# A GpSimd cast put on ScalarE in two of eight MLP steps of a long-convolution and ELU-MLP kernel

## The chip, the cores and the metric

The kernel runs on one core of one Trainium2 chip. The metric is the device time of one execution in microseconds, as the median of several runs. A core has a matrix engine (TensorE, PE in the profile; its weight loads are shown apart as PEld), VectorE (DVE), ScalarE (ACT), GpSimd (POOL) and SyncE (SP), which here only issues DMAs. Each engine takes its instructions in the order in which the program issues them, and waits on semaphores where an operand comes from another engine.

## What is computed

The reference convolves a gated signal with a long generated filter (by FFT, over 12480 positions, 4 batches, 128 channels), gates the result with x, and puts each of the 49920 rows through an MLP with an ELU:

```python
h_filt = (np.maximum(pos_emb @ w1, 0.0) @ w2) * np.exp(-0.01 * pos)[:, None]
u = x * v
y = irfft(rfft(u, n=2 * S, axis=1) * rfft(h_filt, n=2 * S, axis=0)[None], n=2 * S, axis=1)[:, :S]
t = (x * y).reshape(B * S, D)                      # 49920 x 128
h = t @ w_in                                       # 128 -> 2048
g = np.where(h > 0.0, h, np.exp(np.minimum(h, 0.0)) - 1.0)
out = g @ w_out                                    # 2048 -> 128
```

## The kernel before

**Precision.** Every matmul operand is split in two parts, a high one rounded to the format fp32r (`_h`) and the rest (`_l`). A product is then three matmuls, `hi*hi`, `hi*lo` and `lo*hi` (`mm3`, lines 53 to 55). So each operand costs a cast, which rounds it, and a subtraction, which makes the rest. For the MLP's activations g these are line 575 (`g_h`, a cast on GpSimd) and line 581 (`g_l = g - g_h`, on VectorE). The helper `copy` (line 57 and 58) is a ScalarE activation with the function Copy; all its uses show as L58.

**Stages.** First the weights are prepared and the forward and inverse FFT of batch 0 are done (about 530 us, with the filter's own transform in between). Then comes the MLP of all four batches, and beside the MLP of batch p, for p = 0, 1, 2, the FFT work of batch p + 1 (`stage1`, `stage2`), cut into small units that a generator yields. The MLP of batch 3 stands alone.

**The MLP.** It runs over 120 blocks of 416 rows (30 to a batch, batch by batch), and in each block over eight steps c = 0 to 7; a step handles 256 of the 2048 hidden columns. `run` (line 499) writes the order out by hand; what a step s issues, in this order, is:

- `up_proj(s)`: six matmuls into the PSUM tile `fps`, of which there are two; then two ScalarE activations, `n = relu(-h)` (L565) and `n = exp(-n)` (L566), each over 128 x 832;
- `split_lo(s - 2)`: `g_l` (L581, VectorE);
- `elu(s)`: `g = max(n - 1, h)` on VectorE (L572), which is the last reader of `fps`; then the cast `g_h` (L575, GpSimd);
- `down_proj(s - 4)`: six matmuls that add to the PSUM tile `ops`, of which there is one. After the last step of a block, so in the step with c = 3 of the next block, ScalarE copies `ops` to `o_sb` (L58). The next step opens the accumulation of the next block in the same PSUM tile;
- one or two units of the next batch's FFT (`SHARE = 1.08`): ScalarE copies, VectorE products and splits, GpSimd additions (`p<-p`, L431 and L432), matmuls into the two PSUM tiles of `psx`;
- things done once a block: c = 0 the inverse transform of the next block (`conv_out`) and the loads of the one three ahead; c = 1 a store; c = 2 `split_b(j + 2)`; c = 3 `transp(j + 1)`, with the ScalarE copy `t_h` and the VectorE subtraction `t_l`; c = 6 `finish(j - 1)`.

**What is special in batch 0.** Its inverse FFT was written in one part, so `split_b` makes the two parts on the core: a ScalarE copy `b<-b` of 104 x 1024 (L527 in the code, L58 in the profile) and a GpSimd subtraction (L529, also `b<-b`). For the later batches both parts come from memory and `split_b` does nothing.

**Buffers** that the steps below touch: `fps` 2, `ops` 1, `psx` 2, the tile `m` for `conv_out`, `transp` and `finish` 1; in SBUF n 2, g 3, `g_h` and `g_l` 5 each.

Of the kernel before, what the change touches and what calls it, by code (L numbers as in the profile page):

```python
# [38 lines left out]
def fftconv_gate_elu_mlp_kernel(ctx: ExitStack, tc: tile.TileContext, x, v, pos_emb, w1, w2,  # L39
                                w_in, w_out, dft, ident, window, tab, out):  # L40
    nc = tc.nc
# [15 lines left out]
    def copy(out, in_):  # L57
        nc.scalar.activation(out=out, in_=in_, func=ACTF.Copy)  # L58
# [427 lines left out]
    class Mlp:  # L486
# [12 lines left out]
        def run(self, side, alone):  # L499
            blocks = [(b, w, n) for b in range(NB) for w in range(2) for n in range(NG)]  # L500
# [68 lines left out]
            def elu(j, c):  # L569
                ps, n = gs[j, c]  # L570
                g = self.ep.tile([128, 2, NT], F32, tag="g", name="g", bufs=3)
                nc.vector.scalar_tensor_tensor(out=g, in0=n, scalar=-1.0, in1=ps[:, :, :NT],  # L572
                                               op0=ALU.add, op1=ALU.max)
                g_h = self.gp.tile([128, 2, NT], F32R, tag="g_h", name="g_h")
                nc.gpsimd.tensor_copy(out=g_h, in_=g)  # L575
                gs[j, c] = (g, g_h)

            def split_lo(j, c):
# [49 lines left out]
            for s in range(len(steps) + LAG):  # L628
# [7 lines left out]
                if now:  # L636
                    elu(*now)
# [9 lines left out]
                if now:  # L647
                    j, c = now
# [107 lines left out]
```

## Time and profile before

| | us |
|---|---|
| median of 3 runs | 3546.19 (3544.32 to 3550.76) |
| profiled execution, its time | 3553.1 |
| span of the profiled execution, first to last instruction | 3551.3 |
| mean granted TensorE clock | 0.981 |
| MLP steps of batch 0, first to last g | about 530 to 1346 from the span's start |

The rows quoted below come from that one profiled execution. A row of a group reads: line, engine, operation, tile written <- tiles read, shapes, count, then busy us and mean ns of one, then the idle time of the engine just before these instructions and what ended it. A row of the timeline reads: start in us from the span's start, length in us, engine, line, operation, tiles, shapes, and in square brackets the engine's idle time before it with what ended it. A row of the waits reads: who waited, for whom, us in total, times, longest. Line numbers are those of the kernel before.

### The profile page before, as it was taken

To read this page: it belongs to the slowest core of one execution; us is meant where nothing else is said; L and a number is where in the kernel's file an instruction comes from. 1 tells how busy PE (TensorE), PEld (TensorE's weight loads), DVE (VectorE), ACT (ScalarE), POOL (GpSimd) and SP (SyncE) were. 2 spreads that over 40 slices of the span, in tenths; PEclk is the share of its full clock that TensorE was granted. 3 is DMA by queue.
4 is the path that set the end of the run, shared out by engine and by line. 5 is a ranking of instruction groups with operands and counts; after the bars stand their busy time and mean duration, and the time that the engine had idled before them with its cause. 6 is when DMAs were issued, how large, how long until landed. Compare 5 with 4: busy or idle time off the path is not lost.

```text
span 3551.3 us, 53404 instructions
## 1 busy us (share of the span) xinstructions
PE 3394.7 (96%) x18444; PEld 3131.3 (88%) x18444; DVE 3114.3 (88%) x3897; ACT 2410.1 (68%) x3290; POOL 2355.2 (66%) x1622
## 2 busy tenths in 40 slices
PE   7978879999999999999999999999999999999999
PEld 5667758889989998889999998899999999999998
DVE  4549969999999989999999989999999988888887
ACT  3445548766666677876666677776666677777776
POOL 5758857667767766557677656666766656565565
PEclk9879979999999999999999999999999999999999
DMA  6758887667767616778888846778888832222221
GB/s 187 236 170 268 269 245 222 203 175 217 214 191 215 192 50 182 242 213 228 230 241 225 230 124 183 239 215 237 232 240 226 230 102 60 71 59 64 67 59 27
DMA packets 383995, 646.30 MB, mean 182 GB/s; under 512 B 24678, under 2 KB 170438, under 8 KB 374366
## 3 DMA queue, kind: packets, MB, share of 16 engines
q1 hardware_dynamic: 383305, 642.73, 63.8%
q8 instruction: 147, 2.41, 0.3%
q14 instruction: 122, 1.00, 0.1%
q10 hardware_dynamic: 421, 0.16, 0.0%
HBM read 412.76 MB, written 230.03 MB: 181 GB/s over the span
## 4 chain that ended last, share of the span: by engine, by line
PE 59%; DVE 10%; DMA 7%; issue 4%; ACT 1%; POOL 1%; SPq 1%; POOLq 0%; DVEq 0%; ACTq 0%
PE fps L53 8%; PE fps L55 8%; PE fps L54 8%; PE ops L53 7%; PE ops L54 7%; PE ops L55 7%; DMA al<-a_d 3%; DVE g_l L581 3%; PE bps L450 3%; DVE g L572 2%; DMA vt<-in_v_dram 2%; PE xps L53 2%; PE xps L55 2%; PE xps L54 2%; PE yps L53 1%
## 5 line engine op out<-in xcount | busy, mean ns | idle before, releaser
L575 POOL CAST g_h<-g 128x832 fp32r<-128x832 f32 x960 | 1228.3, 1283 | 961.0 <-DVE g L572 960.1
L565 ACT ACTIVATE n<-fps 128x832 f32<-128x832 f32 x960 | 831.9, 867 | 737.9 <-PE fps L55 725.1
L572 DVE SCALAR_TENSOR_TENSOR g<-n,fps 128x832 f32<-128x832 f32 x960 | 974.4, 1015 | 224.2 <-ACT n L566 218.2
L581 DVE TENSOR_TENSOR g_l<-g,g_h 128x832 fp32r<-128x832 f32 x960 | 1111.4, 1158 | 18.3 <-POOL g_h L575 18.3
L566 ACT ACTIVATE n<-n 128x832 f32<-128x832 f32 x960 | 864.6, 901 | 30.4
L53 PE MATMUL fps<-t_h,wi_h 128*128 128x416 f32 x1920 | 715.8, 373 | 22.1 <-DVE g L572 20.9
L53 PE MATMUL ops<-g_h,wo_h 128*128 128x416 f32 x1920 | 677.9, 353 | 0.8 <-ACT o_sb L58 0.3
L54 PE MATMUL ops<-g_l,wo_h 128*128 128x416 f32 x1920 | 675.2, 352 | 0.7 <-DVE g_l L581 0.7
L55 PE MATMUL fps<-t_h,wi_l 128*128 128x416 f32 x1920 | 675.8, 352 | 0.0
L55 PE MATMUL ops<-g_h,wo_l 128*128 128x416 f32 x1920 | 675.8, 352 | 0.0
L54 PE MATMUL fps<-t_l,wi_h 128*128 128x416 f32 x1920 | 675.0, 352 | 0.0
L431 POOL TENSOR_TENSOR p<-p 120x768 f32<-120x768 f32 x204 | 478.9, 2348 | 77.9 <-DVE p L425 58.4
L53 PEld LDWEIGHTS fps<-t_h,wi_h 128*128 128x128 f32 x1920 | 362.4, 189 | 55.9 <-DVE g L572 36.1
L54 PEld LDWEIGHTS fps<-t_l,wi_h 128*128 128x128 f32 x1920 | 364.4, 190 | 13.3 <-DVE t_l L554 0.3
L53 PEld LDWEIGHTS ops<-g_h,wo_h 128*128 128x128 f32 x1920 | 361.8, 188 | 7.1 <-POOL g_h L575 2.1
L54 PEld LDWEIGHTS ops<-g_l,wo_h 128*128 128x128 f32 x1920 | 362.5, 189 | 4.2 <-DVE g_l L581 1.4
L55 PEld LDWEIGHTS ops<-g_h,wo_l 128*128 128x128 f32 x1920 | 361.5, 188 | 4.1
L55 PEld LDWEIGHTS fps<-t_h,wi_l 128*128 128x128 f32 x1920 | 361.8, 188 | 3.2
L423 DVE TENSOR_TENSOR p<-xps,f 120x512 f32<-120x512 f32 x416 | 283.0, 680 | 14.1 <-DMA f<-f_d 5.1
L432 POOL TENSOR_TENSOR p<-p 120x256 f32<-120x256 f32 x204 | 249.5, 1223 | 16.0
L450 PE MATMUL bps<-p,t 120*120 120x256 f32 x832 | 220.4, 387 | 35.4 <-POOL p L432 26.6
L358 DVE TENSOR_TENSOR tl<-t,th 120x360 fp32r<-120x360 f32 x208 | 211.2, 1016 | 27.4 <-ACT th L58 27.3
(96 smaller groups left out, 4946.2 us busy)
## 6 DMA issues: line engine op xcount, KB each, us to landing
a_d<-a_sb SPq DMA_DIRECT2D x90, 832.0 KB
al<-a_d SPq DMA_DIRECT2D x156, 480.0 KB
f<-f_d SPq DMA_DIRECT2D x312, 240.0 KB
b_d<-b_sb SPq DMA_DIRECT2D x156, 480.0 KB
b<-b_d SPq DMA_DIRECT2D x90, 832.0 KB
t<-in_tab_dram SPq DMA_DIRECT2D x208, 281.2 KB
xt<-in_x_dram SPq DMA_DIRECT2D x60, 416.0 KB
vt<-in_v_dram SPq DMA_DIRECT2D x60, 416.0 KB
```

Source lines behind the costliest of these rows:

```text
L53: nc.tensor.matmul(out=ps, lhsT=hi, rhs=bh, start=start, stop=False)
L54: nc.tensor.matmul(out=ps, lhsT=hi, rhs=bl, start=False, stop=False)
L55: nc.tensor.matmul(out=ps, lhsT=lo, rhs=bh, start=False, stop=stop)
L423: nc.vector.tensor_tensor(out=p[:, :, :2], in0=ps[:, :, 0:1, :].to_broadcast([RI, TG, 2, D]), in1=f[:, :, r], op=ALU.mult)
L431: e.tensor_tensor(out=q, in0=q, in1=p, op=ALU.add)
L432: e.tensor_tensor(out=q[:, :, 1], in0=q[:, :, 1], in1=q[:, :, 2], op=ALU.add)
L450: nc.tensor.matmul(out=ps[:, o], lhsT=t[:, o, 3 * N2:], rhs=y[:, o, :2], start=True, stop=True)
L565: nc.scalar.activation(out=n, in_=ps[:, :, :NT], func=ACTF.Relu, scale=-1.0)
L566: nc.scalar.activation(out=n, in_=n, func=ACTF.Exp, scale=-1.0)
L572: nc.vector.scalar_tensor_tensor(out=g, in0=n, scalar=-1.0, in1=ps[:, :, :NT], op0=ALU.add, op1=ALU.max)
L575: nc.gpsimd.tensor_copy(out=g_h, in_=g)
L581: nc.vector.tensor_tensor(out=g_l, in0=g, in1=g_h, op=ALU.subtract)
```

## The change

In `elu`, for blocks of batch 0 and the steps c = 2 and c = 3, the cast of g is issued as a ScalarE copy in place of the GpSimd cast. It keeps its place in the program: right after the VectorE instruction that makes g, ahead of `down_proj`, of the FFT units and of `split_b` or `transp` of the same step. All other steps keep the cast on GpSimd. 60 of 960 casts are moved.

```diff
@@ -572,7 +572,10 @@
                 nc.vector.scalar_tensor_tensor(out=g, in0=n, scalar=-1.0, in1=ps[:, :, :NT],
                                                op0=ALU.add, op1=ALU.max)
                 g_h = self.gp.tile([128, 2, NT], F32R, tag="g_h", name="g_h")
-                nc.gpsimd.tensor_copy(out=g_h, in_=g)
+                if blocks[j][0] == 0 and c in (2, 3):
+                    copy(g_h, g)
+                else:
+                    nc.gpsimd.tensor_copy(out=g_h, in_=g)
                 gs[j, c] = (g, g_h)
```

## The prediction

> **What bounds the kernel now.** I read the page first, for how full each engine is, then the busy time by stretches, for where the first batch's MLP differs from the later ones.
>
> ```profile
> PE 3394.7 (96%) x18444; PEld 3131.3 (88%) x18444; DVE 3114.3 (88%) x3897; ACT 2410.1 (68%) x3290; POOL 2355.2 (66%) x1622
> ...
> L575 POOL CAST g_h<-g 128x832 fp32r<-128x832 f32 x960 | 1228.3, 1283 | 961.0 <-DVE g L572 960.1
> ```
>
> TensorE (PE) is the engine that is nearly always busy. ScalarE (ACT) and GpSimd (POOL) are both about two thirds busy, and the cast of g on POOL usually waits for VectorE (DVE) to make g. The averages invite the change: neither engine looks full. The stages say more. First the instructions that make g, 240 to a batch, then all engines in stretches: the middle of batch 0 (blocks 1 to 24, with the FFT of batch 1 beside them), its last five blocks (no FFT left), and the middle of batch 2. Columns: busy us and count of each engine, clock, DMA share, GB/s.
>
> ```profile
> 530.00:1346.60 816.60, 242.90 (x240) 0.99 0.67 186
> ...
> 2141.70:2933.00 791.30, 243.33 (x240) 1.00 0.75 212
> ```
>
> ```profile
> 555.00:1240.00 685.00, 654.10 (x3618) 612.25 (x3618) 663.49 (x803) 478.53 (x641) 498.50 (x330) 1.00 0.73 204
> 1240.00:1346.00 106.00, 105.24 (x561) 99.66 (x561) 88.21 (x93) 80.30 (x100) 71.89 (x44) 1.00 0.27 71
> ...
> 2160.00:2830.00 670.00, 660.43 (x3660) 621.13 (x3661) 632.87 (x810) 473.79 (x637) 442.47 (x308) 1.00 0.81 230
> ```
>
> Batch 0 takes 816.6 us and batch 2, with the same MLP, 791.3: 25.3 us more. In the middle of batch 0, DVE is busy 663.5 of 685 us (97%) and PE idles 685 - 654.1 = 30.9 us, 1.3 us in each of 24 blocks; in batch 2 it idles 9.6 us of 670. So there is something to win in batch 0, at most about those 30.9 us. What PE waits for there, and the mean length of the matmul that opens an up projection beside that of one inside it:
>
> ```profile
> PE fps L53 <- DVE g L572: 14.6, 16, 1.5
> ...
> PE ops L53 <- ACT o_sb L58: 0.3, 1, 0.3
> ```
>
> ```profile
> L53 PE MATMUL fps<-t_h,wi_h 128*128 128x416 f32 x387 | 146.8, 379 | 14.7 <-DVE g L572 14.6
> ...
> L54 PE MATMUL fps<-t_l,wi_h 128*128 128x416 f32 x386 | 135.9, 352 | 0.0
> ```
>
> Half of the idle time is the up projection waiting for g, which frees its PSUM buffer; the wait for o_sb is next to nothing. A matmul that had to wait is also recorded longer: 379 against 352 ns, 27 ns x 387 = 10.4 us, 0.4 us a block. So PE has about 1.3 + 0.4 = 1.7 us a block in the middle that a delay can fall into, and 106 - 105.24 = 0.76 us in all five last blocks together.
>
> **The change, part by part.** I write 13.2 for step c=2 of block 13. Sixty casts (30 blocks, steps 2 and 3) leave POOL and become ACT copies. POOL loses 60 x 1.28 us; that by itself is worth nothing to the end, since POOL is busy 73% in this stretch. The copy's price: no row shows 128x832 from g, but the second activation below has that shape, both ends in SBUF, and takes 0.90 us; the bounds are the 0.50 us of o_sb (416 columns) and the 1.04 us of b (1024 columns, 104 partitions). I take 0.9.
>
> The copy's wait decides more than its length. It is issued straight behind n of the same step, and must wait until DVE has made g from that n. ACT then does nothing, and everything behind the copy stands: at step 2 the copy b<-b for block j+2 and the next step's n; at step 3 o_sb, the FFT's copies, t_h and the next n. Here is ACT, then DVE, POOL and PE around steps 13.2 and 13.3 (start, length):
>
> ```profile
> 908.57 0.90 ACT L566 ACTIVATE n<-n 128x832 f32<-128x832 f32 x1
> 909.37 1.04 ACT L58 ACTIVATE b<-b 104x1024 fp32r<-104x1024 f32 x1
> 910.66 0.87 ACT L565 ACTIVATE n<-fps 128x832 f32<-128x832 f32 x1 [0.24 <-PE fps L55]
> 911.56 0.90 ACT L566 ACTIVATE n<-n 128x832 f32<-128x832 f32 x1
> 912.36 0.50 ACT L58 ACTIVATE o_sb<-ops 128x416 f32<-128x416 f32 x1
> 912.76 0.59 ACT L58 ACTIVATE b_sb<-bps 120x512 fp32r<-120x512 f32 x1
> 913.23 0.52 ACT L58 ACTIVATE t_h<-tps 128x416 fp32r<-128x416 f32 x1
> 914.18 0.87 ACT L565 ACTIVATE n<-fps 128x832 f32<-128x832 f32 x1 [0.43 <-PE fps L55]
> ```
>
> ```profile
> 909.76 1.01 DVE L572 SCALAR_TENSOR_TENSOR g<-n,fps 128x832 f32<-128x832 f32 x1
> ...
> 912.56 1.01 DVE L572 SCALAR_TENSOR_TENSOR g<-n,fps 128x832 f32<-128x832 f32 x1
> ...
> 916.95 1.75 DVE L358 TENSOR_TENSOR tl<-t,th 120x360 fp32r<-120x360 f32 x1
> ```
>
> ```profile
> 910.84 0.88 POOL L575 CAST g_h<-g 128x832 fp32r<-128x832 f32 x1 [2.12 <-DVE g L572]
> ...
> 915.11 3.20 POOL L529 TENSOR_TENSOR b<-b,b 104x1024 fp32r<-104x1024 f32 x1
> ```
>
> ```profile
> 913.98 0.35 PE L53 MATMUL ops<-g_h,wo_h 128*128 128x416 f32 x1
> ...
> 915.83 0.35 PE L53 MATMUL fps<-t_h,wi_h 128*128 128x416 f32 x1
> ```
>
> ACT has only 0.24 us idle between its first n here and the n of 914.18, bar 0.43 at the end: steps 2 and 3 are the two in which ACT is locally full, with b, o_sb and t_h. Replay, with starts spaced as in the rows (0.8 behind an n, 0.95 behind b, 0.4 behind o_sb) and 0.1 us from DVE to the next engine (910.77 to 910.84 above): g 13.2 ends at 909.76 + 1.01 = 910.77; the copy starts at 910.85 instead of b at 909.37; b at 911.65; n 13.3 at 912.6 (was 910.66), its second half ends at 914.4; g 13.3 runs from 914.45 to 915.45 (was 912.56 to 913.57); the second copy starts at 915.55; o_sb at 916.35 (was 912.36), ending at 916.85. The first matmul of the next output accumulation, at 913.98 now, writes the single PSUM buffer that o_sb empties. It starts at 916.9: PE stalls 2.9 us, in a place where it had 913.98 - 912.86 = 1.1 us to spare.
>
> What is late next: t_h at about 917.2 instead of 913.2, n 13.4 at 917.7 or later instead of 914.18, and so g 13.4 at 919.5 to 920 against 916.01. Its consumer, the up projection of 13.6, has itself been pushed 2.9 us by PE's own stall, so this is mostly the same delay and not a second one. The tables and loads in SP's queue stand behind stores of b_sb that come some 3 us later; they are issued a block or more ahead of use, and I cost them at nothing (3 us once a block, if that lead weren't there).
>
> The last five blocks, without FFT work, replayed from 27.2 (ACT; DVE; PE):
>
> ```profile
> 1290.27 0.90 ACT L566 ACTIVATE n<-n 128x832 f32<-128x832 f32 x1
> 1291.08 1.04 ACT L58 ACTIVATE b<-b 104x1024 fp32r<-104x1024 f32 x1
> 1292.03 0.85 ACT L565 ACTIVATE n<-fps 128x832 f32<-128x832 f32 x1
> 1292.91 0.91 ACT L566 ACTIVATE n<-n 128x832 f32<-128x832 f32 x1
> 1293.72 0.49 ACT L58 ACTIVATE o_sb<-ops 128x416 f32<-128x416 f32 x1
> ```
>
> ```profile
> 1291.21 1.02 DVE L572 SCALAR_TENSOR_TENSOR g<-n,fps 128x832 f32<-128x832 f32 x1 [0.33 <-ACT n L566]
> ...
> 1293.85 1.02 DVE L572 SCALAR_TENSOR_TENSOR g<-n,fps 128x832 f32<-128x832 f32 x1 [0.68 <-ACT n L566]
> ```
>
> ```profile
> 1294.36 0.42 PE L53 MATMUL ops<-g_h,wo_h 128*128 128x416 f32 x1
> ```
>
> The copy starts at 1292.3, b at 1293.1, n 27.3 at 1294.05 and is done at 1295.85, g 27.3 ends at 1296.9, the second copy starts at 1297.0, o_sb runs from 1297.8 to 1298.3, and the matmul of 1294.36 moves to 1298.35: 4.0 us. Blocks 28 and 29 load no further block of batch 0, so they have no b copy (about 0.95 us) and lose 3.0.
>
> Sum: a middle block stalls 2.9 to 4.0 us; I take 3.4, since many of them have one FFT copy more in that queue than 13.2 has. Less the 1.7 us of idle time that it may fall into: 1.7 us x 24 = 41 us. The last five: 3 x 4.0 + 2 x 3.0 - 0.8 = 17 us. Block 0 has no o_sb of an earlier block at its step 3 and is left at nothing. Together +58 us. The profiled execution took 3553.1 us (span 3551.3), 6.9 above the median of 3546.19; it would become 3611, and the median 3604.
>
> The other sign is contention between POOL and DVE. In the rows above, tl took 1.75 us while POOL's b<-b ran to 918.31. The stretch's own row for the subtraction that makes g_l:
>
> ```profile
> L581 DVE TENSOR_TENSOR g_l<-g,g_h 128x832 fp32r<-128x832 f32 x211 | 268.0, 1270 | 3.2 <-POOL g_h L575 3.2
> ```
>
> At 1270 ns against the 1015 ns of g in the same shape, 211 of them lose about 54 us of DVE time. The Trainium skill, SBUF — State Buffer, section "Who interferes with whom", says that a VectorE instruction with two SBUF inputs and a GpSimd one that reads SBUF exclude each other, while ScalarE has ports of its own; this speaks for the change, and tl and g_l against POOL's rows agree. By that rule alone, a quarter of the casts gone would save a quarter of 54, some 13 us, and the sum would end below the time before.
>
> **The rivals.** First, faster: ACT's waits are hidden and POOL's relief counts. For it speaks that batch 0 is 25.3 us longer than batch 2 and that DVE is 97% full and slowed beside POOL. Price: up to 25 us, so 3521. It decides if o_sb is done before PE asks for its buffer, that is, if the chain of two copies costs ACT less than the 1.1 us to spare; the copy alone is 0.9 and g another 1.0, twice. Chance 0.05. Second, no change: the middle gains by quieter DVE (13 us) what the last blocks lose (17): +4 us, 3550. Chance 0.04. Third, only the last blocks lose: in the middle all of the stall falls into waits that are there already, because g 4 and g 5 are late today for DVE's backlog, which drains while ACT is late. +17 us, 3563. PE's 1.7 us of idle time against 3.4 speaks against it. Chance 0.08. That the edit doesn't act is excluded: blocks run batch by batch, so each of the first 30 has both steps.
>
> **How the numbers follow.** The forecast, 3604, has 0.83. Its bounds: the stall 2.9 and 2.4 us of it absorbed (0.5 x 24 + 14 = 26 us: 3572); nothing absorbed and 3.9 us in the middle (94 + 18 = 112 us: 3658). This range leaves out the two first rivals and the third, 0.17 in all. A change of 0.2% is 7 us, about what a measurement of this kernel can tell from none. Faster by more: 0.05; within: 0.04; slower: 0.83 + 0.08 = 0.91.
>
> **What would show it.** Right: waits of PE's first matmul of ops for ACT o_sb of about 2 to 4 us at each block of batch 0, where one of 0.3 us stands now; ACT copies g_h<-g x60 near 0.9 us, with over 1 us of idle time before each, released by DVE g; the stretch of 240 steps 50 to 65 us longer, and batches 1 to 3 unchanged. Wrong: o_sb waits absent, the mean of g_l near 1.0 us and batch 0 under 810 us (the first rival); or the middle's blocks unchanged and only the last five longer (the third).

## The result and the profile after

The kernel with the change takes 3662.84 us (median of 4 runs, 3651.36 to 3674.47) against 3548.48 us of the kernel before in the same comparison: 1.0318 times as long, 95% interval 1.0276 to 1.036. The sign was forecast; the time lies above the range, and the loss is nearly twice the +58 us forecast.

The page of the profiled execution (3667.3 us, span 3665.5), in the lines that answer to those of before:

```profile
PE 3430.6 (94%) x18444; PEld 3165.7 (86%) x18444; DVE 3076.7 (84%) x3897; ACT 2458.4 (67%) x3350; POOL 2277.3 (62%) x1562
...
L578 POOL CAST g_h<-g 128x832 fp32r<-128x832 f32 x900 | 1162.9, 1295 | 1065.5 <-DVE g L572 1061.8
...
L53 PE MATMUL ops<-g_h,wo_h 128*128 128x416 f32 x1920 | 689.9, 359 | 104.1 <-ACT o_sb L58 101.3
```

The last of these lines, in the kernel before:

```profile
L53 PE MATMUL ops<-g_h,wo_h 128*128 128x416 f32 x1920 | 677.9, 353 | 0.8 <-ACT o_sb L58 0.3
```

PE's idle time ahead of the output matmuls was 0.8 us and is 104.1, and nearly all of it is ended by o_sb. PE is also busy for longer, 3430.6 against 3394.7 us, with the same 18444 matmuls. That second number is what the prediction had no term for. It shows best in the MLP of batch 0 alone, from its first g to the first g of batch 1; first the kernel before, then the changed one (us, then busy us and count of PE, PEld, DVE, ACT and POOL, mean clock, DMA share, GB/s):

```profile
534.50:1347.20 812.70, 778.54 (x4264) 728.21 (x4263) 772.18 (x917) 576.56 (x763) 588.28 (x381) 0.99 0.67 186
```

```profile
525.00:1457.60 932.60, 821.95 (x4263) 768.19 (x4262) 734.01 (x917) 625.47 (x823) 508.19 (x321) 0.93 0.59 162
```

This stretch grew by 119.9 us. The rest of the execution gave 9.5 us back ahead of it (525.0 against 534.5) and took about 4 behind it, which makes the 114.2 us between the two profiled executions. Of the 119.9, PE's idle time took 76.5 (932.60 - 821.95 = 110.65 against 34.16), and the same matmuls took 43.4 us more, with the granted clock at 0.93 against 0.99. DVE and POOL are both less busy in total than before.

The waits in that stretch, of the changed kernel (who, for whom, us, times, longest):

```profile
PE ops L53 <- ACT o_sb L58: 101.3, 28, 5.5
...
ACT g_h L58 <- DVE g L572: 82.8, 60, 2.7
...
PE fps L53 <- DVE g L572: 4.1, 5, 1.9
```

Sixty waits of ScalarE for g, 1.4 us each, and 28 waits of PE for o_sb, 3.6 us each. Block 13, of which the prediction made a replay, in the changed kernel (ACT, DVE, PE):

```profile
950.65 0.90 ACT L566 ACTIVATE n<-n 128x832 f32<-128x832 f32 x1
952.95 0.90 ACT L58 ACTIVATE g_h<-g 128x832 fp32r<-128x832 f32 x1 [1.40 <-DVE g L572]
953.76 1.04 ACT L58 ACTIVATE b<-b 104x1024 fp32r<-104x1024 f32 x1
954.70 0.85 ACT L565 ACTIVATE n<-fps 128x832 f32<-128x832 f32 x1
955.58 0.90 ACT L566 ACTIVATE n<-n 128x832 f32<-128x832 f32 x1
957.63 0.90 ACT L58 ACTIVATE g_h<-g 128x832 fp32r<-128x832 f32 x1 [1.15 <-DVE g L572]
958.44 0.50 ACT L58 ACTIVATE o_sb<-ops 128x416 f32<-128x416 f32 x1
```

```profile
951.84 1.01 DVE L572 SCALAR_TENSOR_TENSOR g<-n,fps 128x832 f32<-128x832 f32 x1
...
956.52 1.02 DVE L572 SCALAR_TENSOR_TENSOR g<-n,fps 128x832 f32<-128x832 f32 x1 [1.80 <-ACT n L566]
```

```profile
955.87 0.35 PE L55 MATMUL fps<-t_h,wi_l 128*128 128x416 f32 x1
959.08 0.43 PE L53 MATMUL ops<-g_h,wo_h 128*128 128x416 f32 x1 [2.86 <-ACT o_sb L58]
...
959.94 0.55 PE L53 MATMUL ops<-g_h,wo_h 128*128 128x416 f32 x1
...
962.26 0.55 PE L53 MATMUL fps<-t_h,wi_h 128*128 128x416 f32 x1
```

It goes as replayed: each copy waits for its g and starts 0.1 us behind it, takes 0.90 us, and PE's first output matmul waits 2.86 us where 2.9 was worked out. The new thing is in the last two rows. Behind the wait a matmul takes 0.55 us where it took 0.35. Three stretches of this block follow: the last matmuls ahead of the wait with the wait itself, the twelve matmuls behind it, and what comes next. The clock column (before the DMA share) reads 1.00, 0.56 and 0.91; the trace has the clock at half from 959.4 to 962.9, beginning 0.4 us after PE works again:

```profile
954.84:959.08 4.24, 1.38 (x10) 1.05 (x8) 1.02 (x1) 3.06 (x5) 4.16 (x3) 1.00 0.75 208
959.08:962.26 3.18, 3.18 (x12) 3.10 (x13) 2.81 (x4) 2.79 (x5) 0.45 (x1) 0.56 0.95 281
962.26:965.54 3.28, 3.28 (x19) 3.24 (x19) 2.61 (x5) 1.62 (x2) 1.12 (x1) 0.91 0.23 77
```

The twelve matmuls from the first of ops to the next fps took 915.83 - 913.98 = 1.85 us before and take 962.26 - 959.08 = 3.18 now: 1.3 us on top of the wait in this block.

### The profile page after: what moved, and what is told of

The parts are those of the page before. It is cut to its first block, busy times and chain, and to the rows that moved or that the text cites. A ratio compares the mean times of both kernels' runs of the same rounds, so it can differ in the third digit from the quotient of the medians.

```text
span 3665.5 us, 53309 instructions
## 1 busy us (share of the span) xinstructions
PE 3430.6 (94%) x18444; PEld 3165.7 (86%) x18444; DVE 3076.7 (84%) x3897; ACT 2458.4 (67%) x3350; POOL 2277.3 (62%) x1562
## 4 chain that ended last, share of the span: by engine, by line
PE 70%; DVE 10%; ACT 6%; DMA 5%; issue 4%; POOL 4%; SPq 0%; POOLq 0%; DVEq 0%; ACTq 0%
PE ops L53 8%; PE fps L53 8%; PE fps L55 8%; PE fps L54 8%; PE ops L54 8%; PE ops L55 8%; PE bps L450 4%; DVE g L572 3%; DVE g_l L584 2%; DMA al<-a_d 2%; PE xps L53 2%; PE xps L55 2%; PE xps L54 2%; DMA vt<-in_v_dram 2%; PE yps L54 1%
## 5 line engine op out<-in xcount | busy, mean ns | idle before, releaser
L578 POOL CAST g_h<-g 128x832 fp32r<-128x832 f32 x900 | 1162.9, 1295 | 1065.5 <-DVE g L572 1061.8
L584 DVE TENSOR_TENSOR g_l<-g,g_h 128x832 fp32r<-128x832 f32 x960 | 1086.7, 1132 | 15.9 <-POOL g_h L578 15.9
L53 PE MATMUL ops<-g_h,wo_h 128*128 128x416 f32 x1920 | 689.9, 359 | 104.1 <-ACT o_sb L58 101.3
L54 PE MATMUL ops<-g_l,wo_h 128*128 128x416 f32 x1920 | 684.1, 356 | 0.7 <-DVE g_l L584 0.7
L55 PE MATMUL ops<-g_h,wo_l 128*128 128x416 f32 x1920 | 684.3, 356 | 0.0
L54 PE MATMUL fps<-t_l,wi_h 128*128 128x416 f32 x1920 | 680.0, 354 | 0.0
L54 PEld LDWEIGHTS fps<-t_l,wi_h 128*128 128x128 f32 x1920 | 368.6, 192 | 14.5 <-DVE t_l L554 0.3
L54 PEld LDWEIGHTS ops<-g_l,wo_h 128*128 128x128 f32 x1920 | 369.0, 192 | 4.7 <-DVE g_l L584 1.4
L450 PE MATMUL bps<-p,t 120*120 120x256 f32 x832 | 225.5, 394 | 30.1 <-POOL p L432 26.6
L432 POOL TENSOR_TENSOR p<-p 120x256 f32<-120x256 f32 x204 | 239.3, 1173 | 16.0
L358 DVE TENSOR_TENSOR tl<-t,th 120x360 fp32r<-120x360 f32 x208 | 188.5, 908 | 46.6 <-ACT th L58 44.6
```

The costliest lines, as they stand in the source:

```text
L53: nc.tensor.matmul(out=ps, lhsT=hi, rhs=bh, start=start, stop=False)
L54: nc.tensor.matmul(out=ps, lhsT=hi, rhs=bl, start=False, stop=False)
L55: nc.tensor.matmul(out=ps, lhsT=lo, rhs=bh, start=False, stop=stop)
L432: e.tensor_tensor(out=q[:, :, 1], in0=q[:, :, 1], in1=q[:, :, 2], op=ALU.add)
L450: nc.tensor.matmul(out=ps[:, o], lhsT=t[:, o, 3 * N2:], rhs=y[:, o, :2], start=True, stop=True)
L584: nc.vector.tensor_tensor(out=g_l, in0=g, in1=g_h, op=ALU.subtract)
```

## The experiments

Theory A: the whole loss is PE's wait for o_sb, which stands on ScalarE behind two copies that wait for g, and the halved clock that follows such a wait. Theory B: it is the work of 60 more copies on ScalarE, the busier engine. Theory C: the waits are all, and the clock is no part of it. The table has each run's median, its ratio to the kernel before in the same comparison (3546 to 3548 us) with the interval, and from its profile the MLP of batch 0: length, PE busy, PE idle, idle ahead of the output matmuls, and clock.

| run | median us | ratio | batch 0 us | PE busy | PE idle | ops idle | clock |
|---|---|---|---|---|---|---|---|
| before | 3546.2 | | 812.7 | 778.5 | 34.2 | 0.7 | 0.99 |
| changed | 3662.8 | 1.0318 (1.0276 to 1.0360) | 932.6 | 822.0 | 110.7 | 103.9 | 0.93 |
| step 3 alone | 3594.6 | 1.0122 (1.0098 to 1.0147) | 857.0 | 794.7 | 62.3 | 55.8 | 0.97 |
| step 2 alone | 3582.0 | 1.0084 (1.0061 to 1.0108) | 850.1 | 791.5 | 58.6 | 37.9 | 0.98 |
| o_sb late, no cast moved | 3609.6 | 1.0185 (1.0169 to 1.0202) | 874.4 | 801.8 | 72.6 | 69.8 | 0.96 |
| step 3 behind o_sb | 3599.3 | 1.0161 (1.0137 to 1.0184) | 866.0 | 793.0 | 73.0 | 39.2 | 0.98 |
| changed, wait filled | 3637.1 | 1.0241 (1.0219 to 1.0263) | 901.3 | 853.9 | 47.4 | 40.5 | 0.98 |
| before, same fill | 3568.1 | 1.0063 (1.0047 to 1.0079) | 837.0 | 833.0 | 4.0 | 0.0 | 1.00 |
| copies a step later | 3544.0 | 0.9988 (0.9973 to 1.0003) | 807.7 | 777.3 | 30.4 | 6.9 | 1.00 |
| same, behind o_sb | 3541.3 | 0.9991 (0.9979 to 1.0003) | 807.6 | 779.5 | 28.1 | 0.7 | 0.99 |

The expectations speak of the time at half clock. The traces record the granted clock as 1.0 or 0.5, and in batch 0 it is at 0.5 for 131 us in the changed kernel and 10 before, 55 and 39 with step 3 and step 2 alone, 73 with o_sb late, 31 with step 3 behind o_sb, 32 with the wait filled, 3 in the kernel before with the same fill, and 7 and 11 with the copies a step later. The last column agrees with them, as 2 x (1 - clock) x length, to its rounding.

**One copy at a time.**

```diff
-                if blocks[j][0] == 0 and c in (2, 3):
+                if blocks[j][0] == 0 and c == 3:
```

> Only the cast of step 3 is on ScalarE. Theory A (the loss is PE waiting for o_sb, plus a halved TensorE clock after each long wait): o_sb stands behind one wait for g and one copy, so PE waits about 2 us a block instead of 4 to 5, too short for most clock drops (half clock in batch 0 under 50 us, against 135 us with both casts moved); time 3565 to 3590 us. Theory B (each moved copy fills ScalarE and costs about the same): half the loss, 3605 us, with the clock drops halved too.

```diff
-                if blocks[j][0] == 0 and c in (2, 3):
+                if blocks[j][0] == 0 and c == 2:
```

> Only the cast of step 2 is on ScalarE. Theory A: o_sb is late by the copy and its wait, about 2 us, of which 0.9 us are to spare, so PE waits 1 to 1.5 us a block, nearly all of it hidden in waits that are there already; hardly any clock drops; 3545 to 3570 us. Theory B: half the loss, 3605 us.

PE's waits, step 3 alone and step 2 alone:

```profile
PE ops L53 <- ACT o_sb L58: 55.8, 29, 4.2
```

```profile
PE ops L53 <- ACT o_sb L58: 37.9, 27, 2.3
...
PE fps L53 <- DVE g L572: 9.5, 10, 1.9
```

The waits, 1.9 and 1.4 us each, are those that theory A gave. The times, 3594.6 and 3582.0 us, lie above its ranges by 5 and 12 us. With step 2 alone, less of the waits fell into older ones than expected (37.9 us of wait left PE 24.4 us idler), and in both runs more ran at half clock than expected: 55 us where under 50 was said, and 39 where "hardly any" was. Both runs are also under theory B's 3605. The two losses, 48 and 35 us, add up to 83 and not to the 114 of both: half the copies cost less than half.

**The wait without any copy.** The kernel before, with o_sb itself issued one step later in batch 0, behind the next step's n:

```diff
                 if c == NP - 1:
                     t = self.tq.tile([128, NT], F32, tag="o", name="o_sb")
-                    copy(t, oacc.pop(j))
+                    if j < 2 * NG:
+                        late.append((t, oacc.pop(j)))
+                    else:
+                        copy(t, oacc.pop(j))
...
                     up_proj(*now)
+                if late:
+                    copy(*late.pop())
```

> The kernel before, no cast moved; in batch 0 the copy o_sb is issued one step later on ScalarE, behind the next step's n. Theory A (the loss is PE's wait for o_sb and the clock drops behind it): PE waits about 2.4 us a block, as with one cast moved; half clock in batch 0 40 to 60 us; 3580 to 3610 us. Theory B (the moved copies' work on ScalarE is what costs): as before, 3547 us.

```profile
526.20:1400.60 874.40, 801.79 (x4263) 752.10 (x4262) 765.75 (x917) 578.06 (x763) 583.74 (x381) 0.96 0.62 173
```

```profile
PE ops L53 <- ACT o_sb L58: 72.2, 30, 2.9
```

Not one cast is moved and ACT is as busy as before (578.06 against 576.56 us), yet the kernel loses 63 us. The lateness of o_sb is enough, and theory B falls as an account of the whole. PE's matmuls took 23.3 us more (801.79 - 778.54), with no wait over 2.9 us; 73 us ran at half clock, where 40 to 60 was expected. (The row of the waits holds one wait of batch 1's first block too; the 29 in batch 0 make 69.8 us.)

**The wait filled with work.** The changed kernel, with the six up-projection matmuls of step 4 issued three times into the same tile, just ahead of the wait:

```diff
-                for i in range(2):
+                for i in range(6 if blocks[j][0] == 0 and c == 4 else 2):
+                    i %= 2
                     f = (2 * c + i) * 128
```

> The changed kernel with more work: in batch 0 the six up-projection matmuls of step 4 are issued three times over into the same PSUM tile, just ahead of the place where PE waits for o_sb, 2.26 us of matmuls in a wait of 4.8. Theory A: the wait that is left is too short to halve the clock, half clock in batch 0 falls from 135 us to under 40, and the time falls by 30 to 50 us, to about 3615 to 3630, though PE does 68 us more work. Theory C (the clock is no part of it; the whole loss is waiting): the added matmuls are just hidden, 3660 us, or cost something.

The same edit in the kernel before, as a price of the added work:

> Price of the added matmuls without a wait to fill: the kernel before, with the up projection of step 4 of batch 0 issued three times over. 30 x 12 x 0.188 = 68 us of PE work, of which some falls into PE's idle time there: 3590 to 3615 us. Theory A and C agree here; the run shows what the filled wait of the changed kernel hid.

First the changed kernel with the fill, then the kernel before with it:

```profile
525.20:1426.50 901.30, 853.92 (x4624) 802.69 (x4623) 734.17 (x917) 625.39 (x823) 513.19 (x321) 0.98 0.61 168
```

```profile
527.00:1364.00 837.00, 833.03 (x4623) 795.08 (x4622) 763.77 (x916) 578.34 (x764) 588.06 (x381) 1.00 0.65 181
```

360 more matmuls make the kernel before 22 us slower, less than the 44 to 69 expected: PE is 54.5 us busier there, where 68 was worked out, and 30 us of that fell into idle time (34.2 to 4.0). They make the changed kernel 26 us faster, 3637.1 against 3662.8, less than the 30 to 50 expected. Matmuls add 833.03 - 778.54 = 54.5 us of PE busy time in the one and 853.92 - 821.95 = 32.0 in the other, because the clock there rises from 0.93 to 0.98 (131 us at half clock become 32). Theory C, under which added work can at best be hidden, falls. With fill in both, the change costs 64 us in batch 0 instead of 120.

**The second copy behind o_sb.** Both casts on ScalarE in their own step, that of step 3 issued after `down_proj`:

```diff
-                if blocks[j][0] == 0 and c in (2, 3):
+                if blocks[j][0] == 0 and c == 3:
+                    late.append((g_h, g))
+                elif blocks[j][0] == 0 and c == 2:
                     copy(g_h, g)
...
                     down_proj(*steps[s - LAG])
+                if late:
+                    copy(*late.pop())
```

> Both casts on ScalarE in their own step, but that of step 3 behind o_sb. Theory A: o_sb is late only by the copy of step 2, so PE's wait for it is that of the run with step 2 alone, 1.3 us a block; what the copy of step 3 still delays (t_h, the next n) adds waits for g of step 4; 3580 to 3600 us. If it stays near 3660, it is not o_sb but the late n that costs.

```profile
PE ops L53 <- ACT o_sb L58: 39.2, 27, 2.5
PE fps L53 <- DVE g L573: 16.2, 19, 1.9
```

The wait for o_sb is that of step 2 alone (39.2 against 37.9 us), and the copy of step 3 costs 17 us more (3599.3 against 3582.0), partly as waits of the up projection for g (16.2 against 9.5 us). So that copy delays two things: o_sb, which carries most of its cost, and the next n.

**The same copies without the waits.** Both casts stay on ScalarE, issued one step later, when g is long there; first ahead of `down_proj`, right behind the next n, then behind `down_proj` and so behind o_sb:

```diff
-                    copy(g_h, g)
+                    late.append((g_h, g))
...
                     up_proj(*now)
+                if late:
+                    copy(*late.pop())
```

> Both copies stay on ScalarE but are issued one step later, behind the next step's n, when g has long been made. Theory A: ScalarE waits for nothing, o_sb is 0.9 us late and has about that to spare; PE's wait for o_sb falls under 0.5 us a block and the clock drops go (half clock in batch 0 under 25 us); 3530 to 3555 us. Theory B (the work of 60 copies on ScalarE is what costs): no gain over the changed kernel, about 3660 us.

> The best version that the runs so far point to: both copies on ScalarE one step later and behind o_sb, so that o_sb keeps its time. Theory A: PE's waits for o_sb go to nothing, half clock under 15 us, and what is left is POOL's relief: 3530 to 3545 us, at or a little under the kernel before. Theory B: above 3560 us.

The waits of the first (520 to 1450 us, so with the start of batch 1), and the groups of the second in its batch 0:

```profile
PE fps L53 <- DVE g L573: 12.7, 18, 1.4
...
PE ops L53 <- ACT o_sb L58: 6.2, 9, 1.1
```

```profile
L585 DVE TENSOR_TENSOR g_l<-g,g_h 128x832 fp32r<-128x832 f32 x239 | 297.7, 1246 | 0.0
...
L53 PE MATMUL ops<-g_h,wo_h 128*128 128x416 f32 x474 | 167.8, 354 | 0.7 <-ACT o_sb L58 0.3
...
L58 ACT ACTIVATE g_h<-g 128x832 fp32r<-128x832 f32 x60 | 53.2, 886 | 1.3 <-DVE g L573 1.3
...
L358 DVE TENSOR_TENSOR tl<-t,th 120x360 fp32r<-120x360 f32 x52 | 42.7, 823 | 3.0 <-ACT th L58 3.0
```

The sixty copies are there and take the same time, but ScalarE waits 1.3 us for g in all instead of 82.8, and the loss is gone: 3544.0 and 3541.3 us. Neither can be told from the kernel before (both intervals hold 1), so there is no version here that surely beats it. Against the changed kernel the place of the copy alone is worth some 120 us.

## Why the prediction was right in sign and wrong in size

Two steps of the sum failed: the 1.7 us of old idle time that each stall was said to fall into, and a term that the sum did not have, since it took PE's matmuls at their length of before without a reason.

**Right: the path.** The two copies in a row, the 0.9 us of each, the 0.1 us of hand-over, o_sb behind the second copy, and the single PSUM buffer that o_sb must empty. The stalls were worked out as 24 x 3.4 + 18 = 100 us; the idle time ahead of the output matmuls in batch 0 measures 103.9, of which the last five blocks have 19.1. In the middle the mean is 3.5 us for the 3.4 taken, but the single waits go from 2.0 to 5.5 us, wider than the 2.9 to 4.0 of the replay. Of the tail, block 27, replayed at 4.0 us, from the changed kernel, its wait and the clock right behind it:

```profile
1394.57 0.69 PE L53 MATMUL ops<-g_h,wo_h 128*128 128x416 f32 x1 [4.18 <-ACT o_sb L58]
```

```profile
1395.40:1399.00 3.60, 3.60 (x12) 3.47 (x11) 2.94 (x4) 1.08 (x2) 1.30 (x1) 0.50 0.00 0
```

**Wrong: "Less the 1.7 us of idle time that it may fall into".** That credited 42 us to old idle time. PE's idle time grew by 76.5 us for 103.2 us of new waits, so 27 us were absorbed. Half of that were PE's waits for g, 17.4 us before and 4.1 after in batch 0; the rest were idle times ahead of the FFT's matmuls (7.2 us before and 1.8 after ahead of bps, L450). The 0.4 us a block taken from longer recorded opening matmuls were not absorbed: their mean rose from 377 to 390 ns, while that of the matmuls inside an up projection (L54) rose from 352 to 361, so the excess is no smaller. The groups concerned, in batch 0 of the kernel before and then of the changed one:

```profile
L581 DVE TENSOR_TENSOR g_l<-g,g_h 128x832 fp32r<-128x832 f32 x239 | 299.9, 1255 | 3.2 <-POOL g_h L575 3.2
...
L53 PE MATMUL fps<-t_h,wi_h 128*128 128x416 f32 x480 | 181.1, 377 | 17.7 <-DVE g L572 17.4
...
L358 DVE TENSOR_TENSOR tl<-t,th 120x360 fp32r<-120x360 f32 x52 | 52.6, 1012 | 0.0
```

```profile
L53 PE MATMUL fps<-t_h,wi_h 128*128 128x416 f32 x480 | 187.0, 390 | 4.1 <-DVE g L572 4.1
```

**Missing: the clock.** The sum took every matmul at its length of before. In batch 0 the same matmuls took 43.4 us more. Added up: 58 forecast, 4 us more waiting, 15 us less absorbed and 43 us of slower matmuls make 120, the 119.9 measured. The range's upper end, with 112 us for waits that nothing absorbs, covered every wait that was possible by the replay, but not this. Its lower end gave the last five blocks 14 us without a working; they grew by 24.7 us, and block 0, left at nothing, by 3.1. The trace of before had a hint in its page: the clock row shows 7 to 9 tenths in the first six slices (the first 530 us), where PE is less busy, and 9 throughout behind them.

```profile
PEclk9879979999999999999999999999999999999999
```

**The rivals.** That ScalarE's waits are hidden is refuted by PE's 101.3 us of waits for o_sb. The 25.3 us between batches 0 and 2 were read a little high, since that window opened 4.5 us ahead of batch 0's first g. What the first rival counted on, POOL's relief, was measured without the waits in the last run: tl fell from 1012 ns (52 in batch 0 before) to 823, which is 10 us of DVE time, and g_l from 1255 to 1246 ns, which is 2 us; the kernel's time moved by less than can be told. DVE's busy time in batch 0 fell by 13.4 us in all (772.18 to 758.80), so the 13 us forecast came out in the sum, but from tl and not from the g_l that they were worked out from, and they are not seen in the kernel's time. The slowing of tl beside POOL is there: in the changed kernel the 12 tl without a POOL instruction beside them took 0.53 us, and in the kernel before all 52 had one beside them and took 1.01 us on average. This agrees with the Trainium skill (SBUF — State Buffer, "Who interferes with whom"), by which a VectorE instruction with two SBUF inputs contends with a GpSimd one that reads SBUF. The third rival, that the middle absorbs it all, fails with 24 middle blocks that grew by 3.8 us each: of the 119.9 us the last five and block 0 took 27.8, which leaves 92.1.

**The signs named beforehand** came as said: 60 copies at 898 ns with 1.4 us of idle time before each, o_sb waits of 2 us and more where there were none. Batches 1 to 3 stayed within 4 us in all. The 50 to 65 us longer stretch did not come; it was 120.

## What to carry to other kernels

An instruction moved to an in-order engine brings its wait along: count what stands behind it there until its operand comes, and follow the first of these that another engine needs soon. If the copy may come later, issue it where its operand is ready already; here that took the whole loss away without changing the work. And when a change makes TensorE wait a few microseconds at a regular place, add the slower matmuls behind the wait to the price of the wait.

## What the runs showed of the hardware

The clock of TensorE falls to half behind waits of a few microseconds. In the run with o_sb late, where PE waits 2.4 us on average and 2.9 at most once a block, 73 us of batch 0 run at half clock; with 3.6 us on average, in the changed kernel, 131 us. The Trainium skill, TensorE: Matmul & The Clock Gate, section "HAM oscillation — how this bites in real kernels", gives the rule that there should be no idle gaps of PE above about 3.4 us. The direction agrees; the bound does not, since the waits of 2.9 us and less already cost 23.3 us of slower matmuls here.

Of the 29 waits in batch 0 with o_sb late, nearly all 2.3 to 2.4 us long, 19 bring a drop and 10 don't, and the traces show why. In each of the ten traces the half-clock pieces of batch 0 start on a fixed grid of 3.41 us and last 3.41 us or a multiple of it, and what decides is how long PE idles within one step of the grid. In the ten together, each of the 91 steps behind which the clock fell had at least 1.77 us of idle time (as recorded, with modelled ends of matmuls), and none of the 2293 steps at full clock behind which it stayed had more than 1.84. Two waits of 2.38 us with o_sb late, one step of the grid a row: the first wait lies in one step (3.41 - 1.03 = 2.38 us idle) and the next step is at half clock; the second is cut by the grid into 0.66 and 1.72 us, and the clock stays.

```profile
715.68:719.09 3.41, 1.03 (x6) 0.72 (x6) 3.41 (x4) 3.30 (x6) 3.41 (x3) 1.00 1.00 216
719.09:722.51 3.42, 3.42 (x14) 3.31 (x13) 3.25 (x5) 0.00 (x0) 1.63 (x2) 0.50 1.09 224
...
742.99:746.40 3.41, 2.75 (x19) 2.38 (x17) 3.41 (x3) 2.35 (x4) 2.81 (x2) 1.00 0.99 213
746.40:749.81 3.41, 1.69 (x9) 1.64 (x10) 3.41 (x6) 1.54 (x3) 2.05 (x2) 1.00 0.46 135
749.81:753.23 3.42, 3.42 (x22) 3.33 (x21) 3.42 (x4) 2.27 (x3) 2.94 (x3) 1.00 0.49 128
```

This is read from the traces of one kernel; no run placed a wait on the grid on purpose.

A second thing, which theory A had forecast: 360 matmuls that compute nothing new made the changed kernel 26 us faster. They stand where PE would have idled, and the time at half clock fell from 131 to 32 us.
